# ScalarE clamps the exponents of float64 weights, T is loaded straight to its blocks, deferred stores move behind the first turn

## The chip, the cores and the metric

One core of one Trainium2 chip. The metric is the device time of one execution in microseconds (us), lower is better. A kernel is compared with the kernel before by runs on the same chip. Nine runs of the kernel before spread over some 3 us (1194.2 to 1197.4), so a difference below 1.5 us is at the edge of what these runs can see. The profiled execution of a kernel is one of its runs, and not always a typical one.

## The reference

```python
def reference(x, w_in, w_out, g_ln):            # x: 8 x 3136 x 256, float32
    X = np.fft.fft(np.fft.fft(x, axis=1), axis=2).real     # mixing over positions and features
    h = X.reshape(25088, 256) @ w_in                       # 256 x 1024
    u = h * softmax(h)
    ln = (u - mean(u)) / sqrt(var(u) + 1e-6) * g_ln
    return ln @ w_out                                      # 1024 x 256
```

`w_in` and `w_out` arrive as float64. The kernel turns each value into float32 with integer operations: exponent out of the high word, clamp it, multiply the mantissa back in.

## The kernel before

The batch is worked off in four pairs of batch items. Each pair has a first transform over 98 rows (chunks 0 to 7: VectorE *folds* x, TensorE multiplies by the table F), a *turn* through DRAM (`zd`, then `g`), and 25 *units*: a second transform by the table T, the product with `w_in` (`ps_h`), on VectorE `ev` and `h`, then softmax, layer norm and the product with `w_out` (`Wo`, `ps_o`). The first pair has no earlier work to hide behind, so its folds, the narrowing of both weights, the loading of T and the first turn make a set-up of some 65 us.

```python
    tmp = const.tile([P, NW], I32, name="tmp")
    def narrow(w, raw, outs):                  # one piece, 128 x 512 float64, all on VectorE
        lo, hi, unit = raw[:, 0 : 2 * NW : 2], raw[:, 1 : 2 * NW : 2], tmp
        bits(unit, hi, 20, ALU.logical_shift_right, 0x7FF, ALU.bitwise_and)     # exponent
        bits(unit, unit, -896.0, ALU.add, 0.0, ALU.max)                         # clamp
        bits(unit, unit, 255.0, ALU.min, 2.0 ** 23, ALU.mult)                   # clamp
        ...                                    # sign; mantissa; low word; product
    ...
        turn(first, 0, (nc.sync, nc.gpsimd) * 2)          # g <- zd, first 20 rows of each chunk
        for c in (2, 3, 0, 1, 4, 5, 6, 7):
            keep(first, c, slice(4 * KG, ZR))             # the deferred 80 rows: zd <- z
        weights.place_table()                             # two copies of T on ScalarE
        for h in range(1, 3):
            weights.product_in(h)
        for i in range(KF * D // NW):
            weights.narrow_out(i)
        for t in units[:2]:
            take2(t, transform2(pairs[0], t.k1))          # q <- T, g
            spread(t)                                     # r <- one row of q, to all partitions
```

Of the kernel before, what the change touches and what calls it, by code (L numbers as in the profile page):

```python
# [9 lines left out]
FP32 = mybir.dt.float32  # L10
I32 = mybir.dt.int32
ALU = mybir.AluOpType
ACT = mybir.ActivationFunctionType
# [3 lines left out]
P = 128  # L17


N1, N2 = 49, 64  # L20
NK = N1 // 2 + 1
NH = N2 // 2
PR = 2 * N1
ZR = 4 * NK
CH = 4
NC = NH // CH

KG = 5
# [6 lines left out]
def kernel(  # L35
# [19 lines left out]
    nc = tc.nc  # L55
    B, S, D = x.shape
    FF = moe_w_in.shape[1]
    KF = FF // P
# [8 lines left out]
    const = ctx.enter_context(tc.tile_pool(name="const", bufs=1))  # L67
# [3 lines left out]
    qpool = ctx.enter_context(tc.tile_pool(name="qpool", bufs=4))  # L71
# [3 lines left out]
    fpool = ctx.enter_context(tc.tile_pool(name="fpool", bufs=2))  # L75
# [3 lines left out]
    T = const.tile([P, NK, P], FP32, name="T")  # L79
    Wi = const.tile([P, KD, FF], FP32, name="Wi")  # L80
    Wo = const.tile([P, KF, D], FP32, name="Wo")
    ones = const.tile([P, P], FP32, name="ones")
# [4 lines left out]
    g_ln = const.tile([P, KF], FP32, name="g_ln")  # L87
# [30 lines left out]
    def fold_features(o, i, copy):  # L118
        up, down = i[:, :, 1:128], i[:, :, 255:128:-1]
        nc.vector.tensor_tensor(out=o[:, :, 1:128], in0=up, in1=down, op=ALU.add)  # L120
        nc.vector.tensor_tensor(out=o[:, :, 129:256], in0=up, in1=down, op=ALU.subtract)
        copy(o[:, :, 0:129:128], i[:, :, 0:129:128])  # L122

    def add_mirror(pr, c, engine):

        xa, xb, _ = pr.raw[c]
        n = CH - 1 if c == NC - 1 else CH
        a, rb = xa[:, 0:n, :], xb[:, ::-1, :][:, 0:n, :]
        engine.tensor_tensor(out=a[:, :, 1:D], in0=a[:, :, 1:D], in1=rb[:, :, D - 1 : 0 : -1], op=ALU.add)
        engine.tensor_tensor(out=a[:, :, 0:1], in0=a[:, :, 0:1], in1=rb[:, :, 0:1], op=ALU.add)  # L130

    def fold(pr, c):

        xa, _, x0 = pr.raw.pop(c)
        y = xpool.tile([PR, CH, D], FP32, tag="y", name="y")
        copy = nc.scalar.copy if pr.p else nc.vector.tensor_copy
        fold_features(y, xa, copy)
        pr.y[c] = y
        if c == NC - 1:
            pr.y0 = xpool.tile([PR, 1, D], FP32, tag="y0", name="y0", bufs=1)  # L140
            fold_features(pr.y0, x0, copy)
# [34 lines left out]
    def keep(pr, c, rows):  # L176
        nc.sync.dma_start(out=pr.zd[rows, c * CH : (c + 1) * CH, :], in_=pr.zs[c][rows])
# [20 lines left out]
    def take2(t, ps):  # L198
        t.q = qpool.tile([P, KD * P], FP32, tag="q", name="q")
        nc.scalar.copy(t.q, ps)  # L200

    def spread(t):

        t.r = small.tile([P, 1], FP32, tag="r", name="r")
        nc.sync.dma_start(out=t.r, in_=t.q[0:1, P : 2 * P])
# [141 lines left out]


    NW = 512
    tmp = const.tile([P, NW], I32, name="tmp")  # L350

    def load_piece(w, raw, o, c, j, n):

        if w.dtype == FP32:
            nc.sync.dma_start(out=o[:, j : j + n], in_=w.rearrange("(c p) f -> p c f", p=P)[:, c, j : j + n])
        else:
            src = w.bitcast(I32).rearrange("(c p) f -> p c f", p=P)
            nc.sync.dma_start(out=raw, in_=src[:, c, 2 * j : 2 * (j + n)])

    def bits(o, i, a, op0, b=None, op1=ALU.bypass):  # L360
        nc.vector.tensor_scalar(out=o, in0=i, scalar1=a, scalar2=b, op0=op0, op1=op1)

    def narrow(w, raw, outs):

        if w.dtype == FP32:
            for o, scale in outs:
                nc.vector.tensor_scalar(out=o, in0=o, scalar1=scale, scalar2=2.0 ** 20, op0=ALU.mult, op1=ALU.mult)
            return
        lo, hi, unit = raw[:, 0 : 2 * NW : 2], raw[:, 1 : 2 * NW : 2], tmp

        bits(unit, hi, 20, ALU.logical_shift_right, 0x7FF, ALU.bitwise_and)
        bits(unit, unit, -896.0, ALU.add, 0.0, ALU.max)
        bits(unit, unit, 255.0, ALU.min, 2.0 ** 23, ALU.mult)
        nc.vector.scalar_tensor_tensor(out=unit, in0=hi, scalar=top_bit, in1=unit, op0=ALU.bitwise_and,
                                       op1=ALU.bitwise_or)

        bits(hi, hi, 0xFFFFF, ALU.bitwise_and, 0x100000, ALU.bitwise_or)
        bits(lo, lo, 1, ALU.logical_shift_right)
        m = lo.bitcast(FP32)
        nc.vector.scalar_tensor_tensor(out=m, in0=lo, scalar=2.0 ** -31, in1=hi, op0=ALU.mult, op1=ALU.add)  # L380
        n = NW // len(outs)
        for i, (o, scale) in enumerate(outs):
            r = slice(i * n, (i + 1) * n)
            nc.vector.scalar_tensor_tensor(out=o, in0=m[:, r], scalar=scale, in1=unit[:, r].bitcast(FP32),
                                           op0=ALU.mult, op1=ALU.mult)

    class Weights:


        def load_in(self):  # L390
            raw = fpool.tile([P, 2, FF, 2], FP32, tag="v", name="raw_in", bufs=2)
            raw = raw.rearrange("p a f b -> p (a f b)").bitcast(I32)
            self.w_in = [fpool.tile([P, FF], FP32, tag="h", name="w_in", bufs=2) for _ in range(KD)]
            self.pieces = []
            for c in range(KD):
                for j in range(0, FF, NW):
                    i = 2 * (c * FF + j)
                    self.pieces.append((moe_w_in, raw[:, i : i + 2 * NW], self.w_in[c], c, j, NW))

        def piece_in(self, i):  # L400
            load_piece(*self.pieces[i])

        def narrow_in(self, i):
            w, raw, o, c, j, n = self.pieces[i]
            narrow(w, raw, [(o[:, j : j + n], 2.0 ** -20)])

        def load_tables(self):
            self.Q = fpool.tile([P, KD, D + 1], FP32, tag="ev", name="Q", bufs=1)
# [1 line left out]
            nc.sync.dma_start(out=g_ln, in_=moe_g_ln.rearrange("(c p) -> p c", p=P))  # L410

        def load_table(self):
            self.T = fpool.tile([P, NK, N2], FP32, tag="v", name="T_raw", bufs=2)
            nc.sync.dma_start(out=self.T[0:N2], in_=t_tab)

        def place_table(self):
            for b in range(2):
                r = slice(b * N2, (b + 1) * N2)
                nc.scalar.copy(T[r, :, r], self.T[0:N2])

        def mid(self):

            self.m = w_mid[:, 0 : KD * P].rearrange("p (c k) -> p c k", c=KD)
            for c in range(KD):
                nc.vector.tensor_scalar(out=self.m[:, c, :], in0=ones, scalar1=self.Q[:, c, D:], scalar2=None,
                                        op0=ALU.mult)

        def product_in(self, h):
            ps = ps_h.tile([P, FF], FP32, tag=f"h{h % 2}", name="wps")
# [17 lines left out]
                                  in_=moe_w_out.bitcast(I32).rearrange("(c p) f -> p c f", p=P)[:, c])  # L447

        def scale_out(self):
            nc.vector.tensor_scalar(out=g_ln, in0=g_ln, scalar1=2.0 ** -20, scalar2=None, op0=ALU.mult)  # L450

        def narrow_out(self, i):
            m = NW // D
            narrow(moe_w_out, self.raw[:, 2 * i * NW : 2 * (i + 1) * NW],
                   [(Wo[:, c], g_ln[:, c : c + 1]) for c in range(i * m, (i + 1) * m)])

        def centre(self):

# [35 lines left out]
    with tc.manual_schedule():  # L494
        pairs = [Pair(p) for p in range(NP)]
        first, weights = pairs[0], Weights()
# [19 lines left out]
        nc.vector.memset(ones, 1.0)  # L516
        nc.vector.memset(neg_half, -0.5)
        bits(top_bit, neg_half[:, 0:1].bitcast(I32), 31, ALU.logical_shift_right, 31, ALU.logical_shift_left)
        nc.vector.memset(T, 0.0)
        for c in range(NC):  # L520
            if c < 3:
                for i in ((0, 1), (2,), (3,))[c]:
                    weights.narrow_in(i)
            add_mirror(first, c, nc.vector)
            fold(first, c)
            if c + 6 < NC:
                load(first, c + 6)
            if c == 1:
                weights.load_table()
            elif c == 3:  # L530
                weights.place_out()
                for i in range(2):
                    weights.load_out(i)
                weights.mid()
                weights.scale_out()
            for s in range(CH // 2):
                transform1(first, c * CH // 2 + s)
            if c == 3:
                weights.product_in(0)
        turn(first, 0, (nc.sync, nc.gpsimd) * 2)  # L540
        for c in (2, 3, 0, 1, 4, 5, 6, 7):
            keep(first, c, slice(4 * KG, ZR))
        weights.place_table()
        for h in range(1, 3):
            weights.product_in(h)
        for i in range(KF * D // NW):
            weights.narrow_out(i)

        units = [Unit(p, k1) for p in range(NP) for k1 in range(NK)]
        for t in units[:2]:  # L550
            take2(t, transform2(pairs[0], t.k1))
            spread(t)
        lag = 4
        whole = 4
        for i in range(len(units) + lag):
# [131 lines left out]
```

## Time and profile before

| | before |
|---|---|
| time, median of 6 runs | 1195.58 us (1193.66 to 1196.37) |
| span of the profiled execution | 1192.9 us |
| TensorE busy | 1154.9 us, 97% |
| first matmul | 18.00 us |
| folds over, narrowing of the second weight begins | 47.72 us |
| first turn issued / g used | 52.91 / 60.42 us |
| first `ev`, the start of unit 0 | 66.76 us |

The timeline lines have, in this order, the start in us, the busy time in us, the engine (DVE is VectorE, ACT ScalarE, POOL GpSimd, SPq the sync engine's queue of DMA issues, PE TensorE), the source line, the operation, what it writes `<-` reads, the shape, how many instructions were merged, and in brackets how long the engine had been idle before and what released it. For a DMA issue the busy time is the issue, not the transfer. The prediction below reads the lines of this kernel.

### The profile page before, as it was taken

What the parts mean: (1) busy time and instruction counts of PE and PEld (TensorE: products, weight loads), DVE (VectorE), ACT (ScalarE), POOL (GpSimd) and SP (SyncE); (2) the same over time, 40 slices, a digit from 0 to 9 for tenths busy, and PEclk for the clock granted to TensorE, in tenths of its full rate; (3) what the DMA queues carried; (4) which work ended last, traced back from release to release, by engine and by line L of the source; (5) the groups of instructions that cost most, each with busy time, mean ns of one, the idle gap of its engine ahead of it and who ended that gap; (6) DMA issues with size and microseconds to landing.
All of it is one profiled execution on the core that took longest, in us unless ns stands there. A gap on an engine that the chain in (4) does not pass through costs nothing.

```text
span 1192.9 us, 15912 instructions
## 1 busy us (share of the span) xinstructions
PE 1154.9 (97%) x4720; PEld 876.3 (73%) x4720; DVE 915.5 (77%) x1255; ACT 666.2 (56%) x1382; POOL 494.4 (41%) x964
## 2 busy tenths in 40 slices
PE   2889999999999999999999999999999999999998
PEld 1446777777777777777777777777777777777787
DVE  8889878787778877787777877787776887877780
ACT  1447656565556656565555656565655555555561
POOL 3045444534544443532544443433453344333433
PEclk9989999999999999999999999999999999999999
DMA  9852998978999888777999898897898685776765
GB/s 239 236 139 62 183 165 166 185 138 164 169 172 184 162 165 180 155 139 139 171 181 180 161 173 167 153 172 140 147 187 145 102 149 104 135 126 112 132 108 117
DMA packets 457734, 184.98 MB, mean 155 GB/s; under 512 B 425638, under 2 KB 439534, under 8 KB 457648
## 3 DMA queue, kind: packets, MB, share of 16 engines
q1 hardware_dynamic: 443696, 145.22, 69.6%
q0 software_dynamic: 13952, 38.75, 12.7%
q8 instruction: 38, 0.62, 0.2%
q14 instruction: 48, 0.39, 0.1%
HBM read 44.37 MB, written 38.80 MB: 70 GB/s over the span
## 4 chain that ended last, share of the span: by engine, by line
PE 92%; ACT 1%; issue 1%; DVE 0%; POOL 0%; ACTq 0%; DVEq 0%
PE ps_o L323 57%; PE ps_h L222 28%; PE ps L169 4%; PE ps L194 4%; ACT u L246 0%; ACT h L263 0%; POOL nmean L256 0%; DVE h L236 0%; PE ps_t L303 0%; DVE u L254 0%; ACT uT L308 0%; ACT q L200 0%; DVE uT L579 0%; ACT ot L328 0%; ACT neg L244 0%
## 5 line engine op out<-in xcount | busy, mean ns | idle before, releaser
L323 PE MATMUL ps_o<-Wo,uT 128*128 128x256 f32 x3136 | 693.4, 379 | 0.1
L323 PEld LDWEIGHTS ps_o<-Wo,uT 128*128 128x128 f32 x3136 | 611.6, 196 | 61.9 <-issue 1.4
L222 PE MATMUL ps_h<-Wi,q 128*128 128x512 f32 x800 | 363.3, 597 | 0.7 <-DVE nmax L236 0.6
L254 DVE SCALAR_TENSOR_TENSOR u<-h,u 128x1024 f32<-128x1024 f32 x196 | 240.1, 1226 | 56.8 <-ACT u L246 30.3
L236 DVE CUSTOM_DVE_ANT_0 h<-ev,ps_h 128x1024 f32<-128x1024 f32 x196 | 231.8, 1219 | 50.5 <-PE ps_h L222 35.1
L256 POOL TENSOR_SCALAR nmean<-usum 128x1 f32<-128x1 f32 x196 | 81.2, 415 | 448.0 <-DVE u L254 447.9
L222 PEld LDWEIGHTS ps_h<-Wi,q 128*128 128x128 f32 x800 | 152.9, 192 | 151.4 <-issue 145.1
L263 ACT ACTIVATE h<-u,nmean 128x1024 f32<-128x1024 f32 x196 | 224.7, 1147 | 69.8 <-POOL nmean L256 66.0
L228 DVE SCALAR_TENSOR_TENSOR ev<-w_mid,r,ps_h 128x1024 f32<-128x1024 f32 x100 | 127.8, 1278 | 131.7 <-PE ps_h L222 125.4
L246 ACT ACTIVATE u<-h,neg 128x1024 f32<-128x1024 f32 x196 | 225.2, 1149 | 6.4
L291 DVE STREAM_TRANSPOSE v<-u 128x1024 f32<-128x1024 f32 x192 | 228.3, 1231 | 0.1
L200 ACT COPY q<-ps 128x256 f32<-128x256 f32 x100 | 37.2, 372 | 282.6 <-PE ps L194 234.2
L328 ACT ACTIVATE ot<-ps_o,rs 128x256 f32<-128x256 f32 x196 | 86.8, 462 | 61.1 <-PE ps_o L323 55.0
L335 POOL DMA_INDIRECT out_dram<-ot,idx x96 | 103.1, 1074 | 35.2 <-issue 20.7
L194 PEld LDWEIGHTS ps<-T,g 128*128 128x128 f32 x400 | 60.1, 191 | 51.3 <-issue 50.1
L169 PE MATMUL ps<-y,F 98*100 98x258 f32 (+3 forms) x288 | 72.3, 389 | 24.7 <-DVE y L122 24.7
L278 POOL TENSOR_TENSOR rs<-v,neg_half 128x2 f32<-128x2 f32 (+1 forms) x100 | 82.7, 827 | 7.8
L169 PEld LDWEIGHTS ps<-y,F 98*100 98x100 f32 x288 | 46.2, 179 | 37.1 <-DVE y L122 21.9
L244 ACT ACTIVATE neg<-nmax 128x1 f32<-128x1 f32 x196 | 38.3, 195 | 62.5 <-DVE nmax L236 61.5
L275 POOL TENSOR_SCALAR v<-ssq 128x2 f32<-128x2 f32 (+1 forms) x100 | 23.2, 232 | 114.4 <-ACT h L263 114.4
L194 PE MATMUL ps<-T,g 128*128 128x128 f32 x400 | 60.7, 275 | 3.7 <-DMA g<-zd 3.7
L184 POOL DMA_DIRECT2D g<-zd x78 | 46.6, 607 | 37.4 <-DMA zd<-z_g 28.7
(69 smaller groups left out, 456.1 us busy)
## 6 DMA issues: line engine op xcount, KB each, us to landing
uT<-v SPq DMA_DIRECT2D x752, 128.0 KB
out_dram<-ot SPq DMA_DIRECT2D x100, 128.0 KB
g<-zd POOLq DMA_DIRECT2D x78, 160.0 KB
xa<-in_x_dram SPq DMA_DIRECT2D x28, 392.0 KB
zd<-z SPq DMA_DIRECT2D x24, 400.0 KB
raw_in<-in_moe_w_in_dram SPq DMA_DIRECT2D x4, 512.0 KB
raw_out<-in_moe_w_out_dram SPq DMA_DIRECT2D x2, 1024.0 KB
r<-q SPq DMA_DIRECT2D x100, 0.5 KB
```

Of the source, the lines that this page charges most:

```text
L169: nc.tensor.matmul(o[..., cs], F[:, 2 * t + h, :], i[..., cs], start=first, stop=True, skip_group_check=True)
L194: nc.tensor.matmul(ps[:, h * P : (h + 1) * P], g[:, k, h * P : (h + 1) * P], T[:, k1, :], start=(h == 0), stop=True, skip_group_check=True)
L222: nc.tensor.matmul(ps[:, fs], t.q[:, c * P : (c + 1) * P], Wi[:, c, fs], start=True, stop=True)
L228: nc.vector.scalar_tensor_tensor(out=t.ev, in0=w_mid, scalar=t.r, in1=ps, op0=ALU.mult, op1=ALU.add)
L236: nc.vector.tensor_tensor_reduce(out=t.h[s], in0=t.ev, in1=ps, scale=1.0, scalar=-3.0e38, op0=ALU.subtract if s else ALU.add, op1=ALU.max, ...
L246: nc.scalar.activation(out=t.u[s], in_=t.h[s], func=ACT.Exp, bias=t.neg[:, s : s + 1], accum_out=t.esum[:, s : s + 1])
L254: nc.vector.scalar_tensor_tensor(out=t.u[s], in0=t.h[s], scalar=1.0, in1=t.u[s], op0=ALU.mult, op1=ALU.mult, accum_out=t.usum[:, s : s + 1])
L263: nc.scalar.activation(out=t.h[s], in_=t.u[s], func=ACT.Square, bias=t.nmean[:, s : s + 1], accum_out=t.ssq[:, s : s + 1])
L291: nc.vector.transpose(out=t.batch.v[:, t.w, :, o], in_=t.u[s])
L323: nc.tensor.matmul(ps, uT[:, c, :, s], Wo[:, c, :], start=(c == 0), stop=(c == KF - 1))
L328: nc.scalar.mul(out=t.ot[s], in_=ps, mul=t.rs[:, s : s + 1])
L335: dma = nc.gpsimd.indirect_dma_start(out=out, out_offset=bass.IndirectOffsetOnAxis(ap=idx[:, i : i + 1], axis=0), in_=t.ot[s], in_offset=None)
```

## The change

The clamps leave VectorE: ScalarE makes them of three activations (two Relu and an Identity) beside VectorE's other work, for all pieces but one. For this the exponents are read ahead, into tiles of their own. T is loaded twice straight into its two diagonal blocks, which saves ScalarE two copies. The deferred stores are issued behind the first two transforms and their spreads. The narrowing gets a new order and a tile of its own for the mantissa, and some small operations move from VectorE to ScalarE.

```diff
-    tmp = const.tile([P, NW], I32, name="tmp")
+    mantissa = const.tile([P, NW], I32, name="mantissa")
+    limits = const.tile([P, 3], FP32, name="limits")
@@ exponent: bits(...) into a tile "unit" of qpool, 3 buffers
+    def confine(unit, here=False):
+        if here:
+            bits(unit, unit, -896.0, ALU.add, 0.0, ALU.max)
+            bits(unit, unit, 255.0, ALU.min, 2.0 ** 23, ALU.mult)
+            return
+        u = unit.bitcast(FP32)
+        nc.scalar.activation(out=u, in_=unit, func=ACT.Relu, bias=limits[:, 0:1])
+        nc.scalar.activation(out=u, in_=u, func=ACT.Relu, bias=limits[:, 1:2], scale=-1.0)
+        nc.scalar.activation(out=unit, in_=u, func=ACT.Identity, bias=limits[:, 2:3], scale=-(2.0 ** 23))
@@ T
-            self.T = fpool.tile([P, NK, N2], FP32, tag="v", name="T_raw", bufs=2)
-            nc.sync.dma_start(out=self.T[0:N2], in_=t_tab)
-                nc.scalar.copy(T[r, :, r], self.T[0:N2])
+                nc.sync.dma_start(out=T[r, :, r], in_=t_tab)
@@ the first weight: exponents 0 and 1 before piece 0, 2 before fold 0, 3 before fold 1;
@@ T is issued behind the loads of the second weight (chunk 3) instead of in chunk 1
@@ behind the first turn
-        for c in (2, 3, 0, 1, 4, 5, 6, 7):
-            keep(first, c, slice(4 * KG, ZR))
-        weights.place_table()
+        confine(weights.units[0], True)
+        for i in range(1, 3):
+            confine(weights.units[i])
@@ behind the transforms and spreads of units 0 and 1
+        for c in (2, 3, 0, 1, 4, 5, 6, 7):
+            keep(first, c, slice(4 * KG, ZR))
```

More of the change, by code (lines that the diff above doesn't have):

```diff
@@ L361, in bits, with exponent, narrow @@
         nc.vector.tensor_scalar(out=o, in0=i, scalar1=a, scalar2=b, op0=op0, op1=op1)
-    def narrow(w, raw, outs):
+    def exponent(w, raw):
+        if w.dtype == FP32:
+            return None
+        unit = qpool.tile([P, NW], I32, tag="unit", name="unit", bufs=3)
+        bits(unit, raw[:, 1 : 2 * NW : 2], 20, ALU.logical_shift_right, 0x7FF, ALU.bitwise_and)
+        return unit
+    def confine(unit, here=False):
+        if unit is None:
+            return
+        if here:
+            bits(unit, unit, -896.0, ALU.add, 0.0, ALU.max)
+            bits(unit, unit, 255.0, ALU.min, 2.0 ** 23, ALU.mult)
+            return
+        u = unit.bitcast(FP32)
+        nc.scalar.activation(out=u, in_=unit, func=ACT.Relu, bias=limits[:, 0:1])
+        nc.scalar.activation(out=u, in_=u, func=ACT.Relu, bias=limits[:, 1:2], scale=-1.0)
+        nc.scalar.activation(out=unit, in_=u, func=ACT.Identity, bias=limits[:, 2:3], scale=-(2.0 ** 23))
+    def narrow(w, raw, outs, unit):
         if w.dtype == FP32:
@@ L368, in narrow @@
             return
-        lo, hi, unit = raw[:, 0 : 2 * NW : 2], raw[:, 1 : 2 * NW : 2], tmp
-        bits(unit, hi, 20, ALU.logical_shift_right, 0x7FF, ALU.bitwise_and)
-        bits(unit, unit, -896.0, ALU.add, 0.0, ALU.max)
-        bits(unit, unit, 255.0, ALU.min, 2.0 ** 23, ALU.mult)
+        lo, hi = raw[:, 0 : 2 * NW : 2], raw[:, 1 : 2 * NW : 2]
+        bits(mantissa, hi, 0xFFFFF, ALU.bitwise_and, 0x100000, ALU.bitwise_or)
+        bits(lo, lo, 1, ALU.logical_shift_right)
+        m = lo.bitcast(FP32)
+        nc.vector.scalar_tensor_tensor(out=m, in0=lo, scalar=2.0 ** -31, in1=mantissa, op0=ALU.mult, op1=ALU.add)
         nc.vector.scalar_tensor_tensor(out=unit, in0=hi, scalar=top_bit, in1=unit, op0=ALU.bitwise_and,
                                        op1=ALU.bitwise_or)
-        bits(hi, hi, 0xFFFFF, ALU.bitwise_and, 0x100000, ALU.bitwise_or)
-        bits(lo, lo, 1, ALU.logical_shift_right)
-        m = lo.bitcast(FP32)
-        nc.vector.scalar_tensor_tensor(out=m, in0=lo, scalar=2.0 ** -31, in1=hi, op0=ALU.mult, op1=ALU.add)
         n = NW // len(outs)
@@ L393, in load_in @@
             self.w_in = [fpool.tile([P, FF], FP32, tag="h", name="w_in", bufs=2) for _ in range(KD)]
-            self.pieces = []
+            self.pieces, self.units = [], []
             for c in range(KD):
@@ L401, in piece_in, with exponent_in @@
             load_piece(*self.pieces[i])
+        def exponent_in(self, i):
+            w, raw, o, c, j, n = self.pieces[i]
+            self.units.append(exponent(w, raw))
+            confine(self.units[-1])
         def narrow_in(self, i):
             w, raw, o, c, j, n = self.pieces[i]
-            narrow(w, raw, [(o[:, j : j + n], 2.0 ** -20)])
+            narrow(w, raw, [(o[:, j : j + n], 2.0 ** -20)], self.units.pop(0))
         def load_tables(self):
@@ L412, in load_table @@
         def load_table(self):
-            self.T = fpool.tile([P, NK, N2], FP32, tag="v", name="T_raw", bufs=2)
-            nc.sync.dma_start(out=self.T[0:N2], in_=t_tab)
-        def place_table(self):
             for b in range(2):
                 r = slice(b * N2, (b + 1) * N2)
-                nc.scalar.copy(T[r, :, r], self.T[0:N2])
+                nc.sync.dma_start(out=T[r, :, r], in_=t_tab)
         def mid(self):
@@ L424, in mid @@
             for c in range(KD):
-                nc.vector.tensor_scalar(out=self.m[:, c, :], in0=ones, scalar1=self.Q[:, c, D:], scalar2=None,
-                                        op0=ALU.mult)
+                nc.scalar.mul(out=self.m[:, c, :], in_=ones, mul=self.Q[:, c, D:])
         def product_in(self, h):
@@ L449, in scale_out, with exponent_out @@
         def scale_out(self):
-            nc.vector.tensor_scalar(out=g_ln, in0=g_ln, scalar1=2.0 ** -20, scalar2=None, op0=ALU.mult)
+            nc.scalar.mul(out=g_ln, in_=g_ln, mul=2.0 ** -20)
+        def exponent_out(self, i):
+            self.units.append(exponent(moe_w_out, self.raw[:, 2 * i * NW : 2 * (i + 1) * NW]))
         def narrow_out(self, i):
@@ L454, in narrow_out @@
             narrow(moe_w_out, self.raw[:, 2 * i * NW : 2 * (i + 1) * NW],
-                   [(Wo[:, c], g_ln[:, c : c + 1]) for c in range(i * m, (i + 1) * m)])
+                   [(Wo[:, c], g_ln[:, c : c + 1]) for c in range(i * m, (i + 1) * m)], self.units.pop(0))
         def centre(self):
@@ L518 @@
         bits(top_bit, neg_half[:, 0:1].bitcast(I32), 31, ALU.logical_shift_right, 31, ALU.logical_shift_left)
+        for i, limit in enumerate((-896.0, 255.0, 255.0 * 2.0 ** 23)):
+            nc.vector.memset(limits[:, i : i + 1], limit)
         nc.vector.memset(T, 0.0)
+        weights.exponent_in(0)
+        weights.exponent_in(1)
         for c in range(NC):
-            if c < 3:
-                for i in ((0, 1), (2,), (3,))[c]:
-                    weights.narrow_in(i)
+            if c == 0:
+                weights.narrow_in(0)
+                weights.narrow_in(1)
+            elif c < 3:
+                weights.narrow_in(c + 1)
+            if c < 2:
+                weights.exponent_in(c + 2)
             add_mirror(first, c, nc.vector)
             fold(first, c)
+            if c == NC - 1:
+                for i in range(3):
+                    weights.exponent_out(i)
             if c + 6 < NC:
                 load(first, c + 6)
-            if c == 1:
-                weights.load_table()
-            elif c == 3:
+            if c == 3:
                 weights.place_out()
@@ L533 @@
                     weights.load_out(i)
+                weights.load_table()
                 weights.mid()
@@ L540 @@
         turn(first, 0, (nc.sync, nc.gpsimd) * 2)
-        for c in (2, 3, 0, 1, 4, 5, 6, 7):
-            keep(first, c, slice(4 * KG, ZR))
-        weights.place_table()
-        for h in range(1, 3):
-            weights.product_in(h)
-        for i in range(KF * D // NW):
+        confine(weights.units[0], True)
+        for i in range(1, 3):
+            confine(weights.units[i])
+        weights.product_in(1)
+        weights.narrow_out(0)
+        weights.exponent_out(3)
+        confine(weights.units[-1])
+        weights.product_in(2)
+        for i in range(1, 4):
             weights.narrow_out(i)
```

## The prediction

> **What bounds the kernel now.** I read the page's busy line and slices first, because they say where a saving can be at all.
>
> ```profile
> PE 1154.9 (97%) x4720; PEld 876.3 (73%) x4720; DVE 915.5 (77%) x1255; ACT 666.2 (56%) x1382; POOL 494.4 (41%) x964
> ...
> PE   2889999999999999999999999999999999999998
> ...
> DMA  9852998978999888777999898897898685776765
> ```
>
> TensorE is idle 1192.9 - 1154.9 = 38.0 us in all, and the slices (29.8 us each) put nearly all of it into the first three. From about 100 us on matmuls bound the run and nothing in the diff touches them. So the change can only move the moment at which that steady part starts: the set-up is the question, and 2% (23.9 us) is out of reach unless most of all idle time went. In the same two first slices the DMA engines are 90% and 80% busy.
>
> Next the timeline of TensorE and VectorE over the set-up, which is one relay. First the folding of x (chunks 0 to 7; VectorE folds, TensorE multiplies):
>
> ```profile
> 18.00 3.73 PE L169 MATMUL ps<-y,F 98*100 98x258 f32 x8 [18.00 <-DVE y L122]
> 24.88 3.74 PE L169 MATMUL ps<-y,F 98*100 98x258 f32 x8 [3.15 <-DVE y L122]
> ...
> 36.14 1.22 DVE L129 TENSOR_TENSOR room<-room 98x1020 f32<-98x1020 f32 x1 [1.25 <-DMA room<-in_x_dram]
> ...
> 43.64 0.69 DVE L120 TENSOR_TENSOR y<-xa 98x508 f32<-98x508 f32 x1 [1.01 <-PE ps L169]
> ```
>
> TensorE waits for VectorE's folds, but at chunk 4 (36.14) VectorE itself waits 1.25 us for a load of x. Whatever is saved on VectorE before 36.14 us ends in that wait. Then the narrowing of the second weight and the first unit:
>
> ```profile
> 47.72 0.42 DVE L361 TENSOR_SCALAR tmp<-raw_out 128x512 int32<-128x512 int32 x1
> 48.18 0.89 DVE L361 TENSOR_SCALAR tmp<-tmp 128x512 int32<-128x512 int32 x2
> ...
> 65.40 0.88 DVE L384 SCALAR_TENSOR_TENSOR Wo<-raw_out,g_ln,tmp 128x256 f32<-128x256 f32 x2
> 66.76 1.28 DVE L228 SCALAR_TENSOR_TENSOR ev<-w_mid,r,ps_h 128x1024 f32<-128x1024 f32 x1 [0.48 <-DMA r<-q]
> 68.19 1.22 DVE L236 CUSTOM_DVE_ANT_0 h<-ev,ps_h 128x1024 f32<-128x1024 f32 x1 [0.15 <-DVE ev L228]
> ```
>
> VectorE works without a gap from 47.72 to 66.28; only then can unit 0 start at 66.76. TensorE and the sync queue beside it:
>
> ```profile
> 52.91 0.80 SPq L184 DMA_DIRECT2D g<-zd  x2
> 53.77 0.89 SPq L177 DMA_DIRECT2D zd<-z_u  x2
> ...
> 60.42 1.13 PE L194 MATMUL ps<-T,g 128*128 128x128 f32 x8 [3.67 <-DMA g<-zd]
> ```
>
> The turn (g<-zd) is issued at 52.91 and the eight deferred stores right behind it; g lands at 60.4, and the spread of unit 0 (r<-q), issued behind those stores at 62.62, lands at 66.7. After the wait of 3.67 us the granted clock is 0.50 from 62 to 65 us, and the eight matmuls of the first unit take 5.40 us where they later take 3.60. Two things end nearly together: VectorE's narrowing (66.28) and the spread (66.7).
>
> [...] In the trace's packet records 256 B take 27 ns on average, 1 KB 51 ns, 6400 B 481 ns: a packet of 256 B carries about half as much per ns as one of 1 KB.
>
> **Part 1, the first weight (4 pieces).** A piece loses two clamps on VectorE (2 x 0.445 plus gaps, 0.92 us), 3.7 us over the four pieces. But the exponents are now read ahead, each behind its own load. The completion records of the trace give those loads: piece 1 lands at 8.36, piece 2 at 16.3, piece 3 at 23.0 us. In the new order on VectorE the exponent of piece 1 stands before the work on piece 0, that of piece 2 before the fold of chunk 0, that of piece 3 before the fold of chunk 1. Step by step: exponent 0 at 6.25, exponent 1 waits to 8.36, pieces 0 and 1 need 2 x 3.05 and end at 14.9; exponent 2 waits to 16.3; fold 0 (2.75) ends at 19.5 (18.0 before). Piece 2 to 22.4, exponent 3 waits to 23.0, fold 1 ends at 26.2 (24.9 before). Piece 3 to 29.1, fold 2 ends at 31.8: as before. So TensorE starts about 1.5 us later and has caught up at chunk 2, and chunk 4 still waits for its load at 36.1. Part 1 is worth nothing[...].
>
> **Part 2, the second weight.** From 47.8: three exponents 3 x 0.46 = 1.4; clamps of piece 0 on VectorE 0.9; four narrowings without unit and clamps, 4.61 - 0.46 - 0.92 = 3.23 each, 12.9; exponent 3, 0.46. Sum 15.7, so VectorE is free at about 63.4 instead of 66.28: 2.9 us. Three of the four pairs of clamps have gone to ScalarE, 3 x 0.92 = 2.8 by the other count. ScalarE: nine activations of 0.71, a chain of 2.1 us per piece, in place of two copies of T (2 x 1.53). It takes pieces 1 and 2 from 50.5 to 54.9, Wi to 55.9, piece 3 to 58.1, w_mid to 59.1: each before VectorE asks (55, 58, 61.5 us).
>
> **Part 3, T straight to its blocks.** Before: one load, 64 packets of 6400 B, 64 x 481 / 16 engines = 1.9 us, landing before raw_out. After: two loads of 1600 packets of 256 B, 3200 x 27 / 16 = 5.4 us, behind raw_out in the same queue. raw_out then lands about 1.8 us sooner (47.1 and 49.7 before, about 45.5 and 48), and T ends at about 53.4. The small stores of chunks 3 to 7, on which the turn waits, are queued behind T: the turn is issued at about 54.8, some 1.9 us later.
>
> **Part 4, deferred stores behind the first turn.** These are 8 x 320 KB, 2.6 MB, about 8 us of all engines. Alone, the turn's 640 packets of 1 KB take 640 x 51 / 16 = 2.0 us plus issue and landing, about 4 us instead of 7.5: g at about 59 instead of 60.4. The spread of unit 0 is issued before the stores and lands at about 62.8 instead of 66.7. The stores land at about 70, before turn 1 (issued at 77.2 before) asks for them.
>
> **Sum.** Unit 0 starts when VectorE is free, 63.4 against 66.76: 3.4 us. TensorE's wait for g falls from 3.67 to about 2.2 us. If the clock still drops, the odd half of unit 0 is ready only at 65.6 and the sum over unit 1 is 2.0 us; if it does not, 3.3 us. I take even chances and a small gain at chunk 6: 2.8 us. The steady part moves up by this and keeps it, as it is bound by TensorE. 1195.67 - 2.8 = 1192.9 us, 0.2%.
>
> **Rivals.** (a) T takes over the path: if small packets from DRAM are slower than 27 ns, or if the long lists of T block the sync queue, the turn is issued at 57 or later, g lands at 61 and the gain is nil or a loss of 1 us: 1195 to 1197. For it: one load at 12.93 took 15.1 us to issue[...]. Against it: DMA is idle from 50 to 53.5 before (busy share 0.11, 0.38, 0.00). (b) All waits collapse: fold 0 isn't delayed, the clock stays up, later drops go too (TensorE waits 3.3 us at 85 before): 5 to 7 us, 1189 to 1190.5. Against it stand the landing times of the pieces. (c) ScalarE becomes the bound: its copies of q sit behind w_mid at 59.1, just ahead of g. A microsecond more in its chains would pass straight into unit 0: 1194. (d) The late stores delay turn 1 or the loads of the next batches; 8 us of slack speak against it, and the cost would be 1 to 2 us.
>
> **Range and chances.** (a) and (b) set the ends: 1190.6 to 1195.6. Faster by over 2% would need 23.9 us of 38 idle: 0.01. Slower by as much has no cause in sight: 0.01.
>
> **What will show it.** Right: the first matmul at 19 to 20 us; chunk 4 of VectorE still at about 36 behind a load; narrowing over at about 63.4; g at about 59 with a wait of about 2 us; r landed before VectorE is free; one table load. Wrong: first matmul at or before 17 us (part 1), turn issued after 56 us (part 3), VectorE waiting for ScalarE in the narrowing, or a steady part that gives the gain back.

Passages of the prediction are cut where it is marked, as no trace here shows what they said of the hardware. The sum is 1192.9 us: the mean of 2.0 and 3.3 us is 2.65, and a small gain at chunk 6 makes it 2.8. The ground for the gain at chunk 6 is a guess about the clock. The trace of the kernel before has a granted clock of 1.00 on both sides of 38 us, though matmuls of 98x258 took 653 ns on average up to 38.0 us and 384 ns from 38.2 to 47 us. The 0.71 us of an activation in Part 2 was worked out; the trace of the changed kernel has 0.70 to 0.72 us. In the trace before, the half clock after the wait for g lasted 3.41 us, the one table load took 1.28 us, and from 54 to 60 us the DMA engines moved 318 GB/s, at which the 2.6 MB of Part 4 take 8.2 us.

## More of the kernel before

One more line of its page, on the queue of the sync engine (packets, MB, and the share of the time of all 16 DMA engines), turned out to matter:

```profile
q1 hardware_dynamic: 443696, 145.22, 69.6%
```

Kernels of different calls are compared by their ratios to the kernel before, as the calls ran on two chips.

## The result

| | before | after |
|---|---|---|
| median of 6 runs | 1195.58 us (1193.66 to 1196.37) | 1192.73 us (1191.63 to 1197.30) |
| ratio | | 0.9983, 95% interval 0.9966 to 1.0001 |
| span of the profiled execution | 1192.9 | 1189.9 |

A ratio here is the record's own figure from the fast runs of both kernels, and not quite the ratio of the medians. The predicted 1192.9 us is met, and the sign of the difference was settled by the second set of runs (r_after below, 0.9981, 0.9967 to 0.9995).

The profile after, first the page's lines on busy time, the slices of TensorE and of the DMA engines, and the sync engine's queue:

```profile
PE 1154.2 (97%) x4720; PEld 875.9 (74%) x4720; DVE 907.9 (76%) x1241; ACT 679.0 (57%) x1404; POOL 496.9 (42%) x964
...
PE   2889999999999999999999999999999999999998
...
DMA  9873765756775765654775776664684453544534
...
q1 hardware_dynamic: 446848, 145.63, 48.6%
```

TensorE's work is the same, its idle time 1189.9 - 1154.2 = 35.7 us instead of 38.0. But the sync engine's queue moved 0.3% more bytes in 48.6% of the engines' time instead of 69.6%, over the whole run. Nothing in the diff says why; this comes back below.

Then the timeline of the folds, which answers to the prediction's second fence:

```profile
17.89 3.73 PE L169 MATMUL ps<-y,F 98*100 98x258 f32 x8 [17.89 <-DVE y L122]
...
23.86 3.73 PE L169 MATMUL ps<-y,F 98*100 98x258 f32 x8 [2.24 <-DVE y L122]
...
34.08 1.22 DVE L129 TENSOR_TENSOR room<-room 98x1020 f32<-98x1020 f32 x1 [2.37 <-DMA room<-in_x_dram]
...
35.84 0.69 DVE L120 TENSOR_TENSOR y<-room 98x508 f32<-98x508 f32 x1 [0.45 <-PE ps L169]
```

VectorE still waits at chunk 4 for a load of x, longer than before (2.37 us), but that load is there at 34.08 instead of 36.14. Then the sync engine and TensorE around the first turn:

```profile
36.77 6.12 SPq L440 DMA_DIRECT2D T<-in_t_tab_dram  x2
...
43.00 5.04 SPq L177 DMA_DIRECT2D zd<-z_u  x1
...
48.14 1.63 SPq L177 DMA_DIRECT2D zd<-z_g  x4
...
53.72 0.81 SPq L184 DMA_DIRECT2D g<-zd  x2
...
58.54 1.99 PE L194 MATMUL ps<-T,g 128*128 128x128 f32 x8 [4.40 <-DMA g<-zd]
...
60.32 4.45 PE L222 MATMUL ps_h<-Wi,q 128*128 128x512 f32 x8
```

The second load of T took 5.39 us to issue, one small store behind it 5.04 us, and the last of the small stores, on which the turn waits, landed only just before 53.7. TensorE waited 4.40 us for g. Last, VectorE up to unit 0, and the clock beside it (the windows view: a stretch in us, its length, busy time and instructions of PE, PEld, DVE, ACT, POOL, then the granted clock, the DMA share and GB/s):

```profile
59.99 0.88 DVE L404 SCALAR_TENSOR_TENSOR Wo<-raw_out,g_ln,unit 128x256 f32<-128x256 f32 x2
...
63.15 1.28 DVE L228 SCALAR_TENSOR_TENSOR ev<-w_mid,r,ps_h 128x1024 f32<-128x1024 f32 x1 [2.28 <-PE ps_h L222]
```

```profile
60.00:62.00 2.00, 2.00 (x5) 1.00 (x5) 0.87 (x2) 0.46 (x2) 0.00 (x0) 0.50 0.03 0
```

Unit 0 starts at 63.15 instead of 66.76 us: 3.6 us earlier, predicted were 3.4. But VectorE was done with the narrowing at 60.87 and stood idle for 2.28 us until TensorE, which had got g late and ran at half clock (0.50 from 60 to 62 us), delivered. The number was right; the thing that set it was not the one predicted.

### The profile page after: what moved, and what is told of

It is laid out like the page before. It is cut to its first block, busy times and chain, and to the rows that moved or that the text cites. A ratio compares the mean times of both kernels' runs of the same rounds, so it can differ in the third digit from the quotient of the medians.

```text
span 1189.9 us, 15918 instructions
## 1 busy us (share of the span) xinstructions
PE 1154.2 (97%) x4720; PEld 875.9 (74%) x4720; DVE 907.9 (76%) x1241; ACT 679.0 (57%) x1404; POOL 496.9 (42%) x964
## 3 DMA queue, kind: packets, MB, share of 16 engines
q1 hardware_dynamic: 446848, 145.63, 48.6%
## 5 line engine op out<-in xcount | busy, mean ns | idle before, releaser
L335 POOL DMA_INDIRECT out_dram<-ot,idx x96 | 103.0, 1073 | 35.4 <-issue 20.7
L184 POOL DMA_DIRECT2D g<-zd x78 | 46.7, 608 | 36.6 <-DMA zd<-z_g 30.5
```

Source lines behind the costliest of these rows:

```text
L335: dma = nc.gpsimd.indirect_dma_start(out=out, out_offset=bass.IndirectOffsetOnAxis(ap=idx[:, i : i + 1], axis=0), in_=t.ot[s], in_offset=None)
```

## The experiments

The table collects all twelve runs, and the two traces of the original pair. "Chunk 4" is the time at which VectorE started on chunk 4, which in all fourteen traces had waited for its load of x; "folds" the first operation on the second weight; "turn" its first issue; "ev" the start of unit 0; "256 B" the mean time of a packet of 256 B in the sync engine's queue, in ns, from the packet records. All times are from the profiled execution, except the ratio to the kernel before.

| kernel | median us | ratio (95%) | chunk 4 | folds | turn | ev | 256 B |
|---|---|---|---|---|---|---|---|
| before | 1195.58 | | 36.14 | 47.72 | 52.91 | 66.76 | 27.1 |
| after | 1192.73 | 0.9983 (0.9966 to 1.0001) | 34.08 | 45.11 | 53.72 | 63.15 | 16.7 |
| r_before | 1195.58 | 0.9993 (0.9979 to 1.0006) | 37.69 | 48.36 | 53.34 | 66.79 | 27.0 |
| r_after | 1193.30 | 0.9981 (0.9967 to 0.9995) | 35.60 | 46.61 | 53.36 | 62.81 | 16.6 |
| t_split | 1189.76 | 0.9953 (0.9939 to 0.9966) | 34.48 | 45.48 | 50.23 | 59.95 | 16.5 |
| keep_early | 1198.33 | 1.0028 (1.0014 to 1.0041) | 33.63 | 45.06 | 53.73 | 67.12 | 16.7 |
| clamp_vector | 1194.27 | 0.9983 (0.9970 to 0.9997) | 34.59 | 45.21 | 53.34 | 63.05 | 16.6 |
| only_keep | 1194.48 | 0.9995 (0.9981 to 1.0008) | 35.82 | 46.79 | 51.68 | 65.12 | 27.1 |
| only_t | 1196.83 | 1.0007 (0.9993 to 1.0021) | 37.34 | 48.55 | 58.30 | 72.11 | 27.0 |
| t_late | 1189.96 | 0.9954 (0.9941 to 0.9968) | 36.10 | 47.11 | 51.85 | 61.38 | 16.5 |
| split_clamp_vector | 1192.31 | 0.9974 (0.9961 to 0.9986) | 34.60 | 45.19 | 49.95 | 62.34 | 16.5 |
| keep_t | 1196.11 | 1.0003 (0.9989 to 1.0016) | 35.94 | 46.54 | 56.19 | 66.38 | 27.1 |
| turn_later | 1190.80 | 0.9960 (0.9947 to 0.9974) | 35.96 | 47.49 | 52.23 | 61.78 | 16.6 |
| t_old | 1194.05 | 0.9989 (0.9975 to 1.0004) | 35.54 | 47.13 | 52.08 | 64.80 | 16.4 |

All gave correct results. From "ev" to the end of the span it is 1125.9 (split_clamp_vector) to 1128.6 us (keep_t): what happens before the first `ev` reaches the end, with about 2.7 us of play, whose sources these runs do not separate. A difference of 0.001 in ratio is 1.2 us.

### r_before and r_after: how much of the pair is luck

No edit. The theory at this point was that the gain is made after 45 us, and that the earlier loads in the first pair of traces were luck.

> The kernel before, unchanged, run again for a second trace. In the first pair of traces all loads of the first 36 us landed earlier after the change than before it (piece 2 of the first weight 14.7 against 16.3 us, chunk 4 at 34.1 against 36.1), although nothing in front of them in the queues had changed. If that is luck of the run (theory A), the trace of this one may show chunk 4 anywhere from 34 to 36.5, and the time agrees with the kernel before within 1 us. If it belongs to the change (theory B), chunk 4 stays at 36.0 to 36.3 here.

> The changed kernel, unchanged, run again. Theory A (landing times of the first loads are luck, the gain is made after 45 us): time 2 to 3.5 us below before; in the trace the stretch from the end of the folds to the first ev is 18.0 us (45.1 to 63.15 in the first trace) give or take 0.7, wherever the folds end. Theory B (the change speeds up the first loads): chunk 4 again near 34.1 us.

Chunk 4 of VectorE in r_before and in r_after:

```profile
37.69 1.22 DVE L129 TENSOR_TENSOR room<-room 98x1020 f32<-98x1020 f32 x1 [1.48 <-DMA room<-in_x_dram]
```

```profile
35.60 1.22 DVE L129 TENSOR_TENSOR room<-room 98x1020 f32<-98x1020 f32 x1 [3.23 <-DMA room<-in_x_dram]
```

Both expectations missed in their figures: the load moves by some 1.5 us from run to run in either kernel, and the gap between the kernels remained. The stretch from folds to `ev` in r_after is 62.81 - 46.61 = 16.2 us, not 18.0: turn and `ev` came within 0.4 us of their times in the first trace although the folds ended 1.5 us later. That suggests that the turn waited not for the folds but for the queue of transfers, which the next run tests.

### t_split: only the rows of T that turn 0 needs

```diff
-        def load_table(self):
+        def load_table(self, k=slice(0, KG)):
-                nc.sync.dma_start(out=T[r, :, r], in_=t_tab)
+                nc.sync.dma_start(out=T[r, k, r], in_=t_tab[:, k, :])
@@ behind the deferred stores
+        weights.load_table(slice(KG, NK))
```

> The changed kernel, but only the five rows of T that turn 0 needs are loaded behind raw_out (640 packets of 256 B), the other twenty behind the deferred stores. Theory A: the small stores of chunks 3 to 7 stand behind T in the queue and hold the turn. Then the turn is issued about 3 us earlier relative to the end of the folds (5 to 6 us after it instead of 8.6), TensorE's wait for g falls from 4.4 to under 1.5 us, the first ev starts when VectorE is free, and the time falls a further 1.5 to 2.5 us below the changed kernel. Rival C: the turn waits for the stores' own slow landing, T has nothing to do with it: turn still 8 us or more after the folds, time as the changed kernel within 0.7 us.

```profile
50.23 0.81 SPq L184 DMA_DIRECT2D g<-zd  x2
...
54.85 1.13 PE L194 MATMUL ps<-T,g 128*128 128x128 f32 x8 [0.33 <-ACT unit L383]
...
59.95 1.28 DVE L228 SCALAR_TENSOR_TENSOR ev<-w_mid,r,ps_h 128x1024 f32<-128x1024 f32 x1
```

The turn goes out 4.75 us after the folds instead of 8.6, TensorE no longer waits for g, its clock stays up until 78 us (1.00 from 36 to 60 us, 0.94 in the changed kernel from 48 to 60), and `ev` starts with no wait behind the narrowing. The time falls by 0.0028 to 0.0030, some 3.4 us, more than expected, and this version beats both kernels. The 640 packets of T took 20.2 ns each here, the 3200 in the changed kernel 36.8. T does hold the turn in the changed kernel; rival C falls.

### keep_early: the deferred stores back in their old place

```diff
         turn(first, 0, (nc.sync, nc.gpsimd) * 2)
+        for c in (2, 3, 0, 1, 4, 5, 6, 7):
+            keep(first, c, slice(4 * KG, ZR))
@@ and taken away behind the spreads
```

> The changed kernel with the deferred stores back at their old place, right behind the issue of the first turn. Theory A: they share the engines with g and stand before the spread: from issue to landing of g 7 us instead of 4.8, spread landing about 4 us after its q instead of 2, so first ev 2.5 to 4 us later and the time 2 to 4 us above the changed kernel, near or above before. Rival D (the order of the stores is hidden by VectorE's narrowing): time as the changed kernel within 0.7 us.

```profile
61.03 2.05 PE L194 MATMUL ps<-T,g 128*128 128x128 f32 x8 [6.95 <-DMA g<-zd]
...
67.12 1.28 DVE L228 SCALAR_TENSOR_TENSOR ev<-w_mid,r,ps_h 128x1024 f32<-128x1024 f32 x1 [5.82 <-DMA r<-q]
```

From issue to use of g 7.3 us (4.8 in the changed kernel), then 5.82 us of waiting on VectorE for the spread: 0.0047, 5.6 us, slower than the changed kernel of the same rounds, more than the 2 to 4 expected, and slower than before (the profiled run was the fastest of its five). Without the new place of the stores, the other parts lose.

### clamp_vector and split_clamp_vector: every clamp on VectorE

```diff
-        if here:
+        if True:
             bits(unit, unit, -896.0, ALU.add, 0.0, ALU.max)
```

Once in the changed kernel, once in t_split.

> The changed kernel with every clamp back on VectorE, right behind its exponent; exponents still read ahead, T and the deferred stores as changed. Theory A: VectorE's narrowing of the second weight is 2.5 to 2.8 us longer and takes the place of the turn as the bound of unit 0: first ev waits for nothing of TensorE, time 1 to 2.2 us above the changed kernel. Rival E (ScalarE's part in the clamps gives nothing, as g is the bound anyway): time as the changed kernel within 0.6 us. In the first weight: chunk 4 still waits for its load (before the change 1.3 to 1.5 us, changed 2.4 to 3.2; here 0 to 1).

> The split load of T, with every clamp back on VectorE. Theory A (ScalarE's clamps are hidden in the changed kernel because g comes later than VectorE's narrowing, and count once T no longer holds the turn): first ev at VectorE's end, 2 to 2.8 us later after the folds than in the split, time 1.2 to 2.6 us above the split (1191 to 1192.4 where the kernel before has 1195.5). Rival G (the clamps never count, all the gain is in the transfers): as the split within 0.6 us.

Narrowing and first `ev` in clamp_vector:

```profile
62.25 0.88 DVE L404 SCALAR_TENSOR_TENSOR Wo<-raw_out,g_ln,unit 128x256 f32<-128x256 f32 x2
63.05 1.27 DVE L228 SCALAR_TENSOR_TENSOR ev<-w_mid,r,ps_h 128x1024 f32<-128x1024 f32 x1
```

In the changed kernel the clamps on ScalarE are worth nothing that can be measured: 0.9983 with and without them. The longer narrowing ends at 63.05, just when TensorE was ready in the changed kernel (63.15, 62.81). The traces and the ratios speak for rival E and not for theory A here, though the intervals would leave room for 1 to 2 us. Chunk 4 waited 1.66 us and not 0 to 1. In t_split the same edit:

```profile
61.54 0.88 DVE L404 SCALAR_TENSOR_TENSOR Wo<-raw_out,g_ln,unit 128x256 f32<-128x256 f32 x2
...
62.34 1.27 DVE L228 SCALAR_TENSOR_TENSOR ev<-w_mid,r,ps_h 128x1024 f32<-128x1024 f32 x1
```

It costs 0.0021, 2.5 us, as theory A said (the two ran in different calls; `ev` comes 2.4 us later, 62.34 against 59.95): there the narrowing is the last to arrive. So the part has a value, and the rest of the change hides it.

### only_keep, only_t, keep_t: parts of the change in the kernel before

The kernel before with the stores moved (only_keep), with T straight to its blocks, issued behind the second weight (only_t), and with both (keep_t).

> The kernel before with one part of the change, the deferred stores behind the first transforms. Theory A: g lands about 57 instead of 60.4 us and the spread before VectorE is free, but VectorE's narrowing (66.3) is then the bound: first ev 66.0 to 66.6, so 0.3 to 1 us faster than before and no more; TensorE's wait for g nearly gone. Rival B (the stores' place carries the whole gain): 2 to 3.5 us faster than before.

> The kernel before with one part of the change, T straight to its blocks (issued behind raw_out, no copies on ScalarE). Theory A: the turn is held by T and its g shares the engines with the deferred stores, the spread lands later still: first ev 1.5 to 3.5 us later, time 1.5 to 3.5 us above before. Rival F (T is free, ScalarE's 3.1 us of copies were in the way): same or up to 1 us faster.

> The kernel before with the deferred stores behind the first transforms and T straight to its blocks, so all of the change but the clamps on ScalarE and the exponents read ahead. Theory A: VectorE's narrowing (18.6 us after the folds) and the turn end together, so 0 to 1 us slower than the changed kernel. Theory B (reading ahead lets the first loads land some 2 us earlier; ten traces: chunk 4 at 33.6 to 36.1 with it, 35.8 to 37.7 without): chunk 4 at 35.7 or later here, and 1.5 to 2.5 us slower than the changed kernel.

In only_keep:

```profile
56.52 1.13 PE L194 MATMUL ps<-T,g 128*128 128x128 f32 x8 [0.69 <-DMA g<-zd]
...
65.12 1.27 DVE L228 SCALAR_TENSOR_TENSOR ev<-w_mid,r,ps_h 128x1024 f32<-128x1024 f32 x1
```

The stores alone repair the transfers (g waits 0.69 us instead of 3.67) and gain 0.6 us by the ratio, with an interval that includes no gain at all: VectorE's narrowing, now alone at the end, takes over. only_t costs 0.8 us by the ratio, less than expected and not clear of zero; its profiled run was the slowest of its five (1200.94 us), so the late `ev` of 72.11 is not typical. keep_t, all of the change but clamps and reading ahead, gains nothing (1.0003), and lies 0.0020 above clamp_vector, which differs from it by the exponents read ahead into tiles of their own, the new order and tiles of the narrowing, and two small moves to ScalarE. Theory B of keep_t met its figures. But what is B? The sync queue of keep_t, then of clamp_vector, moved the same packets and bytes:

```profile
q1 hardware_dynamic: 446848, 145.63, 69.8%
```

```profile
q1 hardware_dynamic: 446848, 145.63, 48.1%
```

The last column of the table answers as far as these runs go. Fourteen traces fall in two groups without overlap: 27.0 to 27.1 ns per packet of 256 B in five kernels, 16.4 to 16.7 ns in nine, whatever else was changed in them. Nearly all those packets are the moves uT<-v of the steady part, which no edit touched. The same two groups differ in the start of chunk 4, though they overlap a little there: 35.8 to 37.7 us, mean 36.6, and 33.6 to 36.1, mean 35.0. What the nine share is the exponents read ahead with their tiles, and the new tile `limits`. In the built programs `limits` decides where the later tiles start: it takes 32 bytes ahead of all later pools. The tiles uT, v, the rooms for x of chunks 2 to 5 and the raw weights start 224 bytes past a multiple of 256 in the five kernels (uT at byte 128992 of a partition) and on a multiple of 256 in the nine (135168); the three `unit` buffers add 6144 bytes, which is a multiple of 256.

For the packets of 256 B the traces have 27.0 / 16.5 = 1.64; packets of 1 KB took 50.6 ns before and 48.4 ns after. The larger packets point the same way: all packets of 4096 B that start in the first 33 us took 256 ns on average in the five traces (247 to 265) and 246 ns in the nine (239 to 254), 4% less, again with some overlap. The loads before chunk 4 stretch from 2.5 to 36 us, so an estimate from these packet times is 33.5 x 0.04 = 1.3 us of the 1.6 us by which chunk 4 starts earlier.

What stays open: that alignment is the cause. It goes with the packet times in all fourteen traces, but no run moved the tiles alone, and why the start of a tile should matter was not shown. The kernel before with a dummy tile of 32 bytes would test it, and settle whether reading ahead adds anything. For the packet time of uT<-v it can hardly matter how exponents are read, as in the changed kernel the first of these packets starts at 115.6 us and the narrowing is over at 60.87; for the 2.4 us between keep_t and clamp_vector I have only this argument. It matters, since these 2.4 us are as large as the whole net gain of the change (0.9983, and keep_t without them 1.0003).

### t_late and turn_later: further from t_split

In t_split the rest of T and the deferred stores delayed the spread of unit 2 and turn 1, and TensorE stood still once more:

```profile
79.67 1.11 PE L303 MATMUL ps_t<-ident,u 128*128 128x128 f32 x4 [4.52 <-ACT q L200]
```

t_late issues the rest of T behind the spread of unit 2; turn_later issues turns 1 to 4 one unit later.

```diff
+            if i == 0:                         # t_late, behind spread(nxt)
+                weights.load_table(slice(KG, NK))
```
```diff
-            if 0 < i + 1 < NK // KG:           # turn_later
-                turn(first, i + 1)
+            if 0 < i < NK // KG:
+                turn(first, i)
```

> The split load of T, with the last twenty rows issued behind the spread of unit 2 instead of before it. In the trace of the split the third ev waited 1.0 us for that spread, turn 1 waited 0.8 us for T, and the clock then fell to half for 6.8 us from 78 us. If these are the price of the rest of T: both waits gone, half clock 3.4 us or less, time 0.5 to 1.5 us below the split (1188.3 to 1189.3 where the kernel before has 1195.5). If TensorE makes up for them later: as the split within 0.5 us.

> The split load of T, with turns 1 to 4 issued one unit later (turn 1 behind unit 1). In the split GpSimd issues turn 1 and two loads for 5.6 us before the mean of unit 1 gets its turn; ScalarE waits 3.8 us for that mean, TensorE 4.5 us, and the clock falls to half for 6.8 us from 78 us. Theory H: the mean comes 2.5 to 3.5 us earlier, TensorE's wait falls to about 1.5 us, the clock stays up, time 1 to 3 us below the split (1186.8 to 1188.8 where before has 1195.5). Rival: units 2 to 4 are bound by their own chains and nothing is gained, or unit 5 waits for g: as the split or above.

Neither gained. In t_late the wait of the third `ev` is gone, but turn 1 now waits 0.77 us for the spread, TensorE's wait is 4.51 us and the half clock lasts 6.8 us as before. In turn_later:

```profile
78.17 0.66 PE L303 MATMUL ps_t<-ident,u 128*128 128x128 f32 x4 [1.16 <-ACT q L200]
...
87.48 1.19 PE L194 MATMUL ps<-T,g 128*128 128x128 f32 x4 [4.08 <-ACT h L263]
```

The wait of 4.52 us fell to 1.16, as theory H said, and came back two units later as 4.08 us, with the same 6.8 us of half clock. The rival's outcome came, nothing gained: a wait taken from one unit was paid two units later.

### t_old: T loaded as before

The changed kernel with the single load and the two copies on ScalarE, in their old places.

```diff
-                nc.sync.dma_start(out=T[r, :, r], in_=t_tab)
+            self.T = fpool.tile([P, NK, N2], FP32, tag="v", name="T_raw", bufs=2)
+            nc.sync.dma_start(out=self.T[0:N2], in_=t_tab)      # in chunk 1
+                nc.scalar.copy(T[r, :, r], self.T[0:N2])       # behind the first turn
```

> The changed kernel with T loaded as before (one load of 64 packets of 6400 B behind chunk 1, two copies on ScalarE of 1.53 us each, ahead of the clamps there). Theory A: the turn is free (issued 5 to 6 us after the folds instead of 8.6) but ScalarE is now in the way: its copies of q come 3 us later than in the split, so first ev 0 to 2 us earlier after the folds than in the changed kernel, time 0.5 to 2.5 us below the changed kernel and 1 to 3 above the split. Rival F (ScalarE's copies cost more than T's small packets): above the changed kernel.

```profile
56.75 1.13 PE L194 MATMUL ps<-T,g 128*128 128x128 f32 x8 [1.17 <-ACT unit L384]
60.92 5.86 PE L222 MATMUL ps_h<-Wi,q 128*128 128x512 f32 x8 [3.04 <-ACT q L200]
```

The turn is free again (issued 4.95 us after the folds), but ScalarE's copies of T now stand before the clamps, and TensorE waits 3.04 us for q. The ratio 0.9989 is not distinguishable from the changed kernel's 0.9981 and 0.9983. The intervals overlap; the gain of 0.5 us or more that I expected isn't there. Taking T off ScalarE was right, given the clamps there; loading all of it ahead of the turn was the mistake.

## Why the prediction was right or wrong

**The time** was right: 1192.9 predicted, 1192.73 and 1193.30 measured. So was the premise that only the set-up can move: TensorE's busy time changed by 0.7 us, and from the first `ev` on all traces take the same within 2.7 us. The range was narrower than the rivals that were said to set its ends: (a) reached to 1197, (b) to 1189.

**Part 1 (first weight worth nothing, chunk 4 at 36.1)** is the step that failed. Its landing times were taken from the trace before as fixed. The waits it named are there (exponent 2 waited 1.40 us in the changed kernel), but every load came earlier, piece 2 at 14.7 instead of 16.3, piece 3 at 20.7 instead of 23.0 (completion records of the two traces), so the first matmul started at 17.89, not 19.5, and chunk 4 at 34.08. Over all traces chunk 4 starts 1.6 us earlier on average in the nine kernels. The alignment of their tiles and the exponents read ahead both go with it; which of the two it is was not tested, and the packet times speak for the alignment. The diff shows that only as a tile of three values.

**Part 2 (2.9 us of VectorE)** met its sum with wrong terms. The narrowing after the folds took 60.87 - 45.11 = 15.8 us where 15.7 were predicted, but 1.3 of it was a wait for raw_out that the sum did not have. The work was 14.5 us: in the new order one narrowing takes 3.0 us and not 3.23. ScalarE's activations took 0.70 to 0.72 us, with one table load in the run (1.28 us). For the clamps alone split_clamp_vector shows 2.5 us where nothing hides them. But in the changed kernel they count for nothing that was seen (clamp_vector): the sum made VectorE the last to arrive at unit 0, and TensorE was.

**Part 3 (T makes the turn 1.9 us later)** had the right mechanism and was under-sized. T's packets took 36.8 ns in the changed kernel's trace, where I used the 27 ns of other packets. Where T's blocks start does not explain it: they lie 224 bytes off a multiple of 256 in both kernels, and in t_split 640 packets to the same blocks took 20.2 ns. That the long list in a crowded queue is the reason is a guess, which no run isolates. 3200 x 36.8 / 16 is 7.4 us instead of 5.4. The turn came at 53.72 instead of 54.8 because all before it was earlier; against the folds it was 8.6 us, where t_split has 4.75. By time T costs the changed kernel 3.4 us.

**Part 4 (stores)** was right in direction and is the part without which the change loses: g took 4.8 us from issue to use (about 4 predicted, 7.5 before), and putting the stores back costs 5.6 us.

**The sum** took VectorE's end (Part 2) for the start of unit 0, and what set it was the later of two arrivals: VectorE's narrowing and the transfers with TensorE behind them. That both the wrong bound and the right one stood near 63 us is luck, and so the right number is no proof of the working. TensorE's wait for g was 4.40 us and not 2.2, partly because TensorE was ready 2.6 us earlier.

**Rivals.** Rival (a), T on the path, was what happened, without its figures (turn at 57, g at 61, no gain): the turn came at 53.72 and g at 58.54, as the folds had ended 2.6 us earlier than before. Of (b), fold 0 was indeed not delayed, but the clock fell to half for 3.4 us from 58.6. By the clock records such a stretch lasted 3.41 us before and in the changed kernel, 6.83 in t_split, keep_early and turn_later, and 10.24 in only_t. The length of one wait did not tell whether it came: in r_after, behind a wait of 2.55 us for g, the eight matmuls of the first unit took 4.79 us, in r_before, behind one of 3.15 us, 3.70. Rival (c), ScalarE as the bound, shows only in t_old. Of (d) nothing shows: turn 1 was issued at 74.05, before the change at 77.20.

## What to carry to other kernels

Where two chains meet, cutting the shorter one gains nothing: undo each part in the changed kernel, and again with the other chain cleared, or a good part looks useless and a bad one harmless. Ask of each transfer what stands behind it in its queue: a large one made of small packets that isn't needed yet can delay small ones that are (here the 3200 packets of T put the turn 8.6 us after the folds, where 640 put it 4.75 us after). After an edit look at the byte addresses of the tiles that DMAs touch: here a tile of 12 bytes moved all those behind it, and packets of 256 B took 16.4 to 16.7 ns in the kernels with it and 27.0 to 27.1 in those without, though no run shows that the addresses are the cause.
